# Three-round score visits, table-based roots on ScalarE, and a new recorded order in a two-layer attention and feed-forward kernel

## The chip, the cores and the metric

The kernel runs on one core of a Trainium2 chip. The metric is the time of one execution on the device in microseconds (us). A profile of one execution gives, beside that time, a span: from the first to the last instruction that the profiler recorded. The five engines are named as in the profile: PE (TensorE; its weight loads are listed apart as PEld), DVE (VectorE), ACT (ScalarE), POOL (GpSimd) and SP (SyncE, which here only issues transfers).

## What is computed

Two layers, each of them an attention block and a feed-forward block on 2048 rows of 512 numbers, and both layers with the same weights:

```python
x = x + _A_ref(_layernorm(x), wq, wk, wv, wo, beta)      # attention
x = x + _B_ref(_layernorm(x), w_gate, w_up, w_down)      # gelu(x@w_gate) * (x@w_up) @ w_down
x = x + _A_ref(_layernorm(x), wq, wk, wv, wo, beta)
x = x + _B_ref(_layernorm(x), w_gate, w_up, w_down)
```

The attention has 32 heads of 16 numbers and goes through the rows in four segments of 512. Inside a segment it is causal softmax attention: logits are q times k over 4, those above the diagonal are masked, the softmax is applied to v. Beside it stands a memory: `phi(q) @ M / phi(q) @ z`, where `phi(t)` is `t + 1` for positive t and `exp(t)` else, and M and z gather `phi(k)` and v of the earlier segments. A gate `sigmoid(beta)` for each head mixes the two. The layer norm has no weights: `(x - mean) / sqrt(var + 1e-5)`.

## The kernel before

**Tiling.** A unit of work is one segment of one layer, k = 0 to 7 (k = 0 to 3 are the first layer's segments). Each k has an attention part (class `Att`) and a feed-forward part (class `Ffn`). Everything is kept in SBUF; weights are loaded once. Rows lie 128 to a partition tile, so a segment has four row tiles. A product of 128 x 512 x 512 is four matmuls of 128 columns of weights by 512 columns that gather in one of eight PSUM banks; the down product of the feed-forward part takes 14.

**Two ways to run a product.** `product` (L547 to L559) issues a matmul whole (L559), or as four matmuls of 32 output columns each that run side by side in four quarters of the PE array (L554). The second way, "columns", is taken while the array is already divided like that. Scores need a third way: four heads lie in four groups of 32 rows of the array, and four matmuls of 16 or 32 rows run side by side (L1086), "rows". Each time that the PE goes from one of the three ways to another there is a small gap, and the planner calls that a change of tiling.

**Scores in visits of two rounds.** Each k has 36 rounds of scores. A round is 256 columns in each of four banks, one bank to each of the four row groups. `score` takes two rounds together, a visit: round 0 goes to the first half and round 1 to the second half of four banks. Two exps follow on ACT (L1589), each over two whole banks (128 x 1024). They write probabilities to `pt`, a ring of ten places of one round each. POOL sets the masked probabilities to zero (L1538, L1543), or DVE does by a multiplication (L1548). A flush (L1115) multiplies probabilities by v in columns, and then the places come free. There are 8 x 36 / 2 = 144 visits and 288 exps.

**The layer norm.** In most norms DVE takes mean and variance by two instructions (`bn_stats`, L620, and `bn_aggr`, L623), POOL adds epsilon (L651) and takes the root by a power of -0.5 (L657), DVE writes the normed rows `xn` (L670), and a transposing transfer that SP issues (L520) turns them into `xnT`. For the keys in `BY_PE` (the feed-forward norms of k = 0, 1 and 7) the PE turns them instead (L712, four 128 x 128 transposes for a row tile), and DVE or ACT copies the result out of PSUM. For the three row tiles in `QUICK` (feed-forward norm of k = 1) the sum is taken in the addition itself (`added`, L633), and ACT takes the variance by a Square with a running sum (L640).

**The order.** Nothing is scheduled at run time. While the program is built, `order` runs a planner: it keeps a clock for each engine (class `Clocks` and class `Engine`), with a written duration for each step, and at each point gives the next instruction to the engine whose clock is lowest. Work waits in `items` (PE's products, by due time) and in the engines' `jobs` (by readiness and a slack). A table `POLICY` of some 60 numbers sets due times and slacks, and `STAGES` changes them in stretches of planned time. Each engine then carries out its own instructions in exactly the recorded order and waits at semaphores for the others. Where the planner finds nothing for PE to do but a bank is free, it issues a filler: a 128-column matmul on a tile named `warm` that nobody reads. Twelve of 512 columns also stand at the start, ahead of the first rows.

**The head.** The code before the planner's loop is written by hand: four transfers of x on two queues, statistics of row tiles 0 to 2 on DVE and of row tile 3 on ACT, roots on POOL (L1378), `xn` on DVE, transposes on PE (L722), the first half products of q and k, and the first scores.

## Time and profile before

| what | value |
|---|---|
| median of 3 runs | 537.1 us (536.97 to 538.29) |
| the profiled execution | 536.73 us, span 534.8 us |
| PE busy | 526.8 us of the span |
| DVE, ACT, POOL busy | 432.7, 433.8, 280.2 us |
| granted TensorE clock | 1.00 |

A matmul's duration in the profile holds its way through the array: 512 columns are listed with 380 ns, but in a stream they start some 215 ns apart. So an engine that is listed as busy all the time may still have small gaps in its stream, and a gap of the array is longer than the idle time listed for it. Durations on the other engines also overlap a little from one instruction to the next.

### The profile page before, as it was taken

The page shows a single profiled execution, that of the slowest core. Times are in us where ns is not written, and L with a number is a line of the kernel's source. Part 1 is how long each engine was busy: PE and PEld are TensorE (multiplying, and loading weights), DVE is VectorE, ACT ScalarE, POOL GpSimd, SP SyncE. Part 2 cuts the span into 40 slices and gives each one's busy share as a digit, 9 for nine tenths or more (in the row PEclk, how much of TensorE's full clock was granted, in tenths as well). Part 3 has the DMA queues.
Part 4 walks back from the last instruction along what each step waited for, and adds up shares of the span by engine and source line. Part 5 has one row for each costly group of instructions (what it writes and reads, how often), then busy time and mean ns, then how long its engine had stood idle before and what let it go on. Part 6 is the DMA issues. An engine that isn't in the chain of part 4 may idle for free.

```text
span 534.8 us, 22313 instructions
## 1 busy us (share of the span) xinstructions
PE 526.8 (99%) x9803; PEld 270.1 (51%) x9803; DVE 432.7 (81%) x814; ACT 433.8 (81%) x544; POOL 280.2 (52%) x344
## 2 busy tenths in 40 slices
PE   8999999999999999999999999999999999999997
PEld 4544454555545455545444554545555456545444
DVE  7898899899999998688897889888786797786342
ACT  5999999997998799998999899998879977820320
POOL 4876767385836587337671697816465254100000
PEclk9999999999999999999999999999999999999999
DMA  8345910640122143210130130220231003100001
GB/s 271 67 116 113 242 33 2 171 76 18 34 49 44 24 52 61 43 32 4 43 80 1 26 82 4 42 52 12 63 63 23 1 12 92 24 4 31 11 0 39
DMA packets 72403, 28.83 MB, mean 54 GB/s; under 512 B 56690, under 2 KB 72306, under 8 KB 72306
## 3 DMA queue, kind: packets, MB, share of 16 engines
q1 hardware_dynamic: 72016, 27.15, 23.5%
q8 instruction: 76, 1.25, 1.0%
q10 hardware_dynamic: 290, 0.26, 0.1%
q14 instruction: 21, 0.17, 0.1%
HBM read 9.70 MB, written 2.10 MB: 22 GB/s over the span
## 4 chain that ended last, share of the span: by engine, by line
PE 89%; DVE 5%; ACT 4%; issue 1%; POOL 1%; ACTq 0%; DVEq 0%; POOLq 0%
PE ps L559 43%; PE ps L554 30%; PE ps L1086 8%; PE ps L1115 6%; ACT pt L1589 2%; DVE st L620 1%; DVE gel_sb L1277 0%; ACT wd_sb L545 0%; PE ps L1015 0%; DVE x_sb L1206 0%; DVE byq L1134 0%; DVE e L894 0%; DVE st L1368 0%; DVE xn L670 0%; PE ps L712 0%
## 5 line engine op out<-in xcount | busy, mean ns | idle before, releaser
L1589 ACT ACTIVATE pt<-ps 128x1024 bf16<-128x1024 f32 x288 | 280.3, 1032 | 35.6 <-PE ps L1086 27.2
L1538 POOL TENSOR_SCALAR_AFFINE_SELECT pt<-pt 128x256 bf16<-128x256 bf16 (+1 forms) x192 | 113.9, 606 | 126.5 <-ACT pt L1589 123.1
L1277 DVE TENSOR_TENSOR gel_sb<-gel_sb,ps 128x512 bf16<-128x512 bf16 x112 | 75.6, 683 | 35.6 <-PE ps L559 25.3
L559 PE MATMUL ps<-xnT,wg_sb 128*128 128x512 bf16 x279 | 65.5, 380 | 0.0
L559 PE MATMUL ps<-xnT,wu_sb 128*128 128x512 bf16 x269 | 62.0, 379 | 0.0
L913 POOL TENSOR_SCALAR e<-e 128x512 bf16<-128x512 bf16 x37 | 58.0, 1569 | 2.6 <-ACT e L890 2.0
L1134 DVE STREAM_TRANSPOSE byq<-ps 128x512 f32<-128x512 f32 x64 | 45.3, 707 | 15.5 <-PE ps L1115 14.3
L559 PE MATMUL ps<-wd_sb,gel_sb 128*128 128x512 bf16 (+1 forms) x289 | 56.8, 347 | 0.0
L1206 DVE TENSOR_TENSOR x_sb<-x_sb,ps 128x512 bf16<-128x512 bf16 (+1 forms) x65 | 41.1, 641 | 19.1 <-PE ps L559 15.0
L554 PE MATMUL ps<-wd_sb,gel_sb 128*32 128x512 bf16 (+1 forms) x860 | 49.9, 368 | 0.2 <-issue 0.2
L1543 POOL TENSOR_SCALAR_AFFINE_SELECT pt<-pt 64x1024 bf16<-64x1024 bf16 x28 | 33.4, 1195 | 16.8 <-ACT pt L1589 15.8
L554 PE MATMUL ps<-xnT,wg_sb 128*32 128x512 bf16 x676 | 41.5, 380 | 0.2 <-ACT xnT L545 0.2
L554 PE MATMUL ps<-xnT,wu_sb 128*32 128x512 bf16 x716 | 41.1, 379 | 0.1
L559 PEld LDWEIGHTS <-wg_sb 128*128 128x128 bf16 x279 | 25.7, 98 | 29.7 <-issue 0.9
L559 PEld LDWEIGHTS <-wu_sb 128*128 128x128 bf16 x269 | 25.2, 98 | 29.8 <-issue 0.7
L620 DVE BATCH_NORM_STATS2 st<-x_sb 128x6 f32<-128x512 bf16 x57 | 38.4, 673 | 0.3
L559 PEld LDWEIGHTS <-gel_sb 128*128 128x128 bf16 x289 | 26.8, 98 | 23.2 <-issue 0.9
L1115 PE MATMUL ps<-pt,vaug 128*32 128x256 bf16 (+2 forms) x1344 | 34.8, 238 | 0.0
L544 DVE CAST gel_sb<-ps 128x512 bf16<-128x512 f32 x42 | 28.4, 681 | 6.7 <-PE ps L559 4.0
L1115 PEld LDWEIGHTS <-vaug 128*32 128x32 bf16 x1344 | 27.8, 97 | 10.5 <-issue 1.6
L1336 ACT ACTIVATE gel_sb<-gel_sb 128x2048 bf16<-128x2048 bf16 (+3 forms) x22 | 32.3, 1540 | 0.0
L1086 PEld LDWEIGHTS <-kx 32*128 32x128 bf16 x1120 | 16.6, 92 | 29.0 <-issue 28.4
(152 smaller groups left out, 871.6 us busy)
## 6 DMA issues: line engine op xcount, KB each, us to landing
vz<-vaug SPq DMA_DIRECT2D x14, 136.0 KB, 2.6
wg_sb<-in_B_w_gate_dram SPq DMA_DIRECT2D x8, 224.0 KB, 4.1
wu_sb<-in_B_w_up_dram SPq DMA_DIRECT2D x8, 224.0 KB, 6.4
wd_sb<-in_B_w_down_dram SPq DMA_DIRECT2D x7, 256.0 KB, 4.6
x_sb<-in_A_x_dram SPq DMA_DIRECT2D x3, 512.0 KB, 6.8
out_dram<-x_sb SPq DMA_DIRECT2D x12, 128.0 KB, 1.8
xnT<-xn SPq DMA_TRANSPOSE x48, 2.6
kx<-kf SPq DMA_DIRECT2D x12, 64.0 KB, 2.6
```

The lines of the kernel that those rows point to most:

```text
L554: nc.tensor.matmul(out[r], lhsT=lhsT[:, r], rhs=rhs, start=start, stop=stop, tile_position=(0, 32 * c))
L559: nc.tensor.matmul(out, lhsT=lhsT, rhs=rhs, start=start, stop=stop)
L620: nc.vector.bn_stats(out=self.st6[:, 0, :], in_=x_sb[:, self.tt0 + j, :])
L913: lambda eng: eng.tensor_scalar(out=e[0][:], in0=e[0][:], scalar1=1.0, scalar2=None, op0=ALU.min), summed)
L1086: nc.tensor.matmul(ps_all[:, bank, o + c0:o + c0 + n], lhsT=lhsT, rhs=self.q[rows, b, q0:q0 + n], start=True, stop=True, tile_position=(32 ...
L1115: nc.tensor.matmul(ps()[32 * j:32 * j + 32, q0:q0 + nq], lhsT=va[:, ki * VW + g:ki * VW + g + 32], rhs=pt_all[:, places[t], j, o:o + nq], ...
L1134: nc.vector.transpose(out=(self.byq[:, pars[0], :, :].rearrange("p a c -> p (a c)") if h is None else self.byq[:].rearrange("p u a c -> p ...
L1206: ck.dve.post(ck.made(), slack, (0.15 + 0.00104 * (c1 - c0), lambda: nc.vector.tensor_tensor(out=xt, in0=xt, in1=ps()[:, 0:c1 - c0], op=AL ...
L1277: ck.dve.post(ck.made(), NORMAL, (0.683, lambda: nc.vector.tensor_tensor(out=g, in0=g, in1=ps()[:], op=ALU.mult), lambda t: (ps.read(t), e ...
L1538: nc.gpsimd.affine_select(out=view, in_=view, pattern=[[0, 4], [0, n], [1, C]], compare_op=ALU.is_ge, fill=0.0, base=C, channel_multiplier=-1)
L1543: nc.gpsimd.affine_select(out=view, in_=view, pattern=[[0, 4 * TPS], [1, C]], compare_op=ALU.is_ge, fill=0.0, base=0, channel_multiplier=-1)
L1589: nc.scalar.activation(out=pt_all[:, s0:s0 + 2, 2 * p:2 * p + 2, :].rearrange("p r h c -> p h r c"), in_=ps_all[:, pair[0]:pair[1] + 1, :] ...
```

## The change

**Visits of three rounds.** With the policy number `triple` on, `score` takes three rounds together. They use six banks (three pairs) and three exps of the same size as before. Of the four row groups, two use banks 4, 2, 2 and 5, 3, 3 of the visit's six, and the other two 0, 0, 4 and 1, 1, 5 (`OWN`; `HIGH` tells which half). Two banks are thus written by two different row groups, one half each, and ahead of the first matmul that goes to such a second half PE waits until its earlier matmul to that bank has ended (`clobber_nop`). `triple` is on in three stretches; the built program has 12 visits of three rounds and 126 of two. `pt` has twelve places in place of ten.

**Roots.** `scales` posts the root to both POOL (as before) and ACT, and the engine that comes to it first in the plan takes it. On ACT it is a Ln with epsilon as bias and an Exp with a scale of -0.5, both of 128 x 2 here. A set of function tables that holds both Ln and Exp is loaded where ACT comes back from gelu.

**Norms.** `QUICK` and `BY_PE` are gone. A policy number (`quick`) says for each feed-forward norm how many row tiles take the sum in the addition and the Square on ACT; all feed-forward norms are rooted in pairs of row tiles; numbers `turn_pe` and `turn_last` say which are turned by PE.

**Head.** ACT takes row tile 0's statistics and DVE those of 1 to 3; the roots are Ln and Exp on ACT for three tiles and then one. The four transposes go to four banks, and ACT and DVE copy them out in turn, with a 256-column `warm` matmul after each. Half products of k and q come after all of them.

**Buffers.** `buf` has five places in place of six, `ab`, `mblk` and `zcols` one in place of two, the reciprocal of the softmax sums is written in place, `bd` is bf16, `warm` shares a place. A flush's first part therefore waits for the unit before it to be turned, not the one before that.

**Loads.** The transfers of wo, w_gate and w_up are planned from 18.04 us on (32.0 before), those of w_down from 59.6 (94.0).

**Planner.** ACT's overlap from one instruction to the next is 0.118 us (0.09 before), DVE's 0.075 (0.07). A new counter, `issue`, counts PE's instructions, and lets the PE clock wait if 256 of them were issued faster than 3.7 us after they were asked for. `POLICY` has new numbers in every place, and `STAGES` thirteen stretches in place of four. Fillers multiply `ident` by itself.

In instructions: PE has 9880 matmuls (9803 before). Transposes of `xn` on PE are 112 (64 before), transposing transfers of `xn` 36 (48 before). Fillers are 22 matmuls, 6 whole and 16 as columns (75 before, 15 whole and 60 as columns). Changes of tiling, counted along PE's order, are 300 (299 before). ACT has 24 Squares (3), 32 small root instructions (none), 16 table loads (14), and 10 fewer evictions of 512 columns. DVE has 39 `bn_stats` (60), 24 additions with a sum (3), and 21 more casts out of PSUM. POOL has 16 roots beside the head's as before, now all of 128 x 2 (14 of the 16 were 128 x 4), the head's two are gone, and there are 4 fewer `min` steps.

The head on ACT, ahead of the first exp, before:

```order
L1383 ACT_TABLE_LOAD
L1383 ACTIVATE pt,shift<-x_sb 128x512
L1384 ACTIVATE pt,mv<-x_sb,shift 128x512
L725 ACTIVATE xnT<-ps 128x4x128 x2
L1409 ACTIVATE macc<-ps 128x32
L1410 ACTIVATE tmp_e_134<-ps 128x32
```

and now (`logs` and `rs` are the two steps of the root):

```order
L1519 ACT_TABLE_LOAD
L1520 ACTIVATE pt,shift<-x_sb 128x512
L1521 ACTIVATE pt,mv<-x_sb,shift 128x512
L1513 ACTIVATE logs<-mv,eps 128x3
L1514 ACTIVATE rs<-logs 128x3
L1513 ACTIVATE logs<-mv,eps 128x1
L1514 ACTIVATE rs<-logs 128x1
L859 ACTIVATE xnT<-ps 128x4x128 x2
L1547 ACTIVATE wd_sb<-ps 128x256
```

The statistics moved from row tile 3 to row tile 0, and four root instructions stand ahead of the copies out of PSUM.

ACT where the first feed-forward norm (k = 0) is turned, before (`e` is a step of phi, `xnT` the copy of the turned rows):

```order
L890 ACTIVATE e<-q 128x512
L1589 ACTIVATE pt<-ps 128x2x2x256 x2
L545 ACTIVATE xnT<-ps 128x4x128 x2
L890 ACTIVATE e<-q 128x512
L1589 ACTIVATE pt<-ps 128x2x2x256 x2
```

and now (`junk` is the Square with the running sum, `ve` and `rs` the root):

```order
L1732 ACTIVATE pt<-ps 128x2x2x256
L760 ACTIVATE junk,mv<-x_sb,mv 128x512
L1732 ACTIVATE pt<-ps 128x2x2x256
L760 ACTIVATE junk,mv<-x_sb,mv 128x512
L780 ACTIVATE ve<-mv,eps 128x2
L786 ACTIVATE rs<-ve 128x2
L1732 ACTIVATE pt<-ps 128x2x2x256
L780 ACTIVATE ve<-mv,eps 128x2
L786 ACTIVATE rs<-ve 128x2
L1732 ACTIVATE pt<-ps 128x2x2x256
```

Squares and roots of the norm stand between single exps on ACT's queue, where before there were exps, a step of phi and the copies alone.

PE in the first segment before, between the 10th and the 12th round of scores (v's product between two whole fillers):

```order
L559 LDWEIGHTS warm
L559 MATMUL ps<-warm 128x128
L559 LDWEIGHTS xnT
L559 MATMUL ps<-wv_sb,xnT 128x512
L559 LDWEIGHTS xnT
L559 MATMUL ps<-wv_sb,xnT 128x512
L559 LDWEIGHTS xnT
L559 MATMUL ps<-wv_sb,xnT 128x512
L559 LDWEIGHTS xnT
L559 MATMUL ps<-wv_sb,xnT 128x512
L559 LDWEIGHTS warm
L559 MATMUL ps<-warm 128x128
```

and now the first fillers of the program, which stand after the 34th round:

```order
L428 LDWEIGHTS wd_sb
L428 MATMUL ps<-wd_sb 128x192
L428 LDWEIGHTS ident
L428 MATMUL ps<-ident 128x128
L428 LDWEIGHTS ident
L428 MATMUL ps<-ident 128x128
L428 LDWEIGHTS xnT
L428 MATMUL ps<-wv_sb,xnT 128x512
```

Before, 42 of the 75 filler matmuls stand ahead of the 13th round; now the 22 that are left stand after the 34th, the 44th and the 57th.

The diff, cut to its core:

```diff
-BY_PE = {("xnTf", 0), ("xnTf", 1), ("xnTf", NK - 1)}
-QUICK = {("xnTf", 1): (0, 1, 2)}
-PT_SLOTS = 10
+VISIT = 3
+PARTS = ((1, 4, 2), (2, 5, 2), (0, 6, 5))
+OWN = ((4, 2, 2), (5, 3, 3), (0, 0, 4), (1, 1, 5))
+HIGH = ((0, 0, 1), (0, 0, 1), (0, 1, 1), (0, 1, 1))
+PT_SLOTS = 12
-BUFS = 6
+BUFS = 5
...
-    flush_wait=4.959, piece_slack=35.752, kb_slack=40.713, mem_slack=-52.285, margin=2.0, qk_due=1.503, e_q=-1.996,
+    rs_pool=-16.958, f_urge=-58.138, quick=4, paired=8, turn_pe=8, turn_last=7, w_at=18.04, w_gap=2.197,
...
-        self.act, self.dve, self.pool, self.sp = Engine(0.09), Engine(0.07), Engine(), Engine()
+        self.act, self.dve, self.pool, self.sp = Engine(0.118), Engine(0.075), Engine(), Engine()
...
+    def issue(self, n=2):
+        for _ in range(n):
+            self.issued += 1
+            at = self.issued % CHUNK
+            if at == CHUNK_ASKED:
+                self.fetching = self.pe + FETCH
+            elif at == CHUNK_END:
+                late = max(0.0, self.fetched - self.pe)
...
+                self.pe += late
+                self.fetched = self.fetching
...
         def scales(self, ready, j0, n):
...
+            def moved(on_pool):
...
+                    nc.scalar.activation(out=self.ve[:], in_=var_in, func=ACT.Ln, bias=eps[:])
...
+            def power():
+                nc.scalar.activation(out=rs(), in_=self.ve[:], func=ACT.Exp, scale=-0.5)
...
+            ck.pool.post(ready, slack + pol.rs_pool, (0.25, lambda: moved(True), None), (1.05, second, told), taken=taken)
+            ck.act.post(ready, slack, (0.29, lambda: moved(False), None), (0.29, power, told), table="exp", taken=taken)
...
         def by_pe(self):
-            return self.key in BY_PE or self.key[0] == "xnTa" and self.key[1] <= pol.pe_turns
+            return (pol.turn_last if self.key[1] == NK - 1 else pol.turn_pe) if self.wide else self.key[1] <= pol.pe_turns
...
+                    if crossed and m == 0 and j == 2:
+                        ck.issue(1)
+                        nc.tensor.clobber_nop([nc.tensor.lower_ap(ps_all[:, i, UNIT:L]) for i in crossed])
...
-                              and (n > 0 or unit < 2 or ("turned", unit - 2) in ev),
+                              and (n > 0 or unit < 1 or ("turned", unit - 1) in ev),
...
-                    if j in self.norm.quick:
+                    if j < pol.quick:
                         self.norm.added(j, ps, self.norm.urge(j))
...
-    first_stats(0)
+    nc.scalar.preload_act_table_set("natural_log_exp_and_others")
+    nc.scalar.activation(out=spare[:, 0, :], in_=x_sb[:, 0, :], func=ACT.Copy, scale=-root / D, accum_out=shift[:])
+    nc.scalar.activation(out=spare[:, 1, :], in_=x_sb[:, 0, :], func=ACT.Square, scale=root, bias=shift[:],
+                         accum_out=n0.mv[:, 0, 1:2])
     first_stats(1)
...
+    first_scale(0, 3)
+    first_scale(3, 4)
...
+            places = [(chosen[j], UNIT * r) if n < VISIT else (chosen[OWN[j][r]], UNIT * HIGH[j][r]) for j in range(4)]
+            a.score_round(t, places, chosen[4:] if r == VISIT - 1 else None)
```

381 lines of the change are left out of this document (243 added, 138 removed).

## The prediction

> **What bounds the kernel now.** I read the page's totals first, then the busy times by stage, then PE's timeline at the places where it has idle time, and last the groups. The totals and the chain that ended last:
>
> ```profile
> PE 526.8 (99%) x9803; PEld 270.1 (51%) x9803; DVE 432.7 (81%) x814; ACT 433.8 (81%) x544; POOL 280.2 (52%) x344
> PE 89%; DVE 5%; ACT 4%; issue 1%; POOL 1%; ACTq 0%; DVEq 0%; POOLq 0%
> ```
>
> PE is listed as busy in all but 8.0 of 534.8 us and carries 89% of the chain. So only two things change the time: work that PE gets or loses, and waits of PE. Where the waits lie is seen by stage (busy us of PE, PEld, DVE, ACT, POOL; the cuts are the first scores, the last exp of the second segment and the last exp of all):
>
> ```profile
> 0.00:11.00 11.00, 9.23 (x59) 4.55 (x60) 8.12 (x28) 5.42 (x13) 3.89 (x16) 1.00 0.84 260
> 11.00:113.40 102.40, 100.02 (x1976) 50.86 (x1974) 91.82 (x181) 98.91 (x127) 72.31 (x85) 1.00 0.48 108
> 113.40:461.70 348.30, 347.30 (x7010) 178.61 (x7010) 295.09 (x545) 311.38 (x382) 202.03 (x241) 1.00 0.20 39
> 461.70:534.80 73.10, 70.28 (x772) 36.12 (x760) 37.64 (x65) 18.06 (x26) 1.94 (x3) 1.00 0.07 17
> ```
>
> PE idles 1.77 us in the head, 2.38 in the first two segments, 1.00 in the other six, and 2.82 at the end, where the last rows are added and sent. ACT is busy 97% of the second stage (98.91 of 102.40) and 89% of the third. So in the first two segments ACT is as full as PE, and later it has room. The waits themselves:
>
> ```profile
> 20.68 0.40 PE L554 MATMUL ps<-warm 128*32 128x128 bf16 x16
> 21.82 0.30 PE L554 MATMUL ps<-warm 128*32 128x128 bf16 x8 [0.19 <-ACT wd_sb L545]
> 24.15 0.22 PE L559 MATMUL ps<-warm 128*128 128x128 bf16 x1 [0.16 <-ACT pt L1589]
> 25.07 0.22 PE L559 MATMUL ps<-warm 128*128 128x128 bf16 x1
> 25.57 0.41 PE L1086 MATMUL ps<-wd_sb 16*128 16x64 bf16 x24 [0.28 <-ACT pt L1589]
> 28.54 1.02 PE L559 MATMUL ps<-xnT,wq_sb 128*128 128x512 bf16 x4 [0.68 <-DVE byq L1134]
> ...
> 74.91 0.66 PE L1015 MATMUL ps<-gel_sb,phik 128*32 128x32 bf16 x64 [0.57 <-ACT pt L1589]
> 76.81 1.48 PE L554 MATMUL ps<-xnT,wg_sb 128*32 128x512 bf16 x24 [0.16 <-ACT xnT L545]
> ```
>
> They stand beside fillers, and ACT releases most. A wait is longer than listed: the filler of 25.07 streams for 0.05 us, and the scores behind it start at 25.57, so the array stood for 0.45 us where 0.28 is listed. The rest, 0.17, is the filler's way through the array. Between 11 and 461.7 us I count 14 starts of PE that come over 0.12 us late beside a plain change of tiling, the first at 21.82 and the last at 454.6 (the eight rows above have six of them). So the array loses 3.4 listed (2.38 + 1.00) + 14 x 0.16 = 5.6 us in waits, and what is not in the head or the end cannot give more than that and the fillers.
>
> **The change, part by part.** The sum is made on the profiled execution, 536.73 us (span 534.8 and 1.9 around it), which lies 0.4 under the median of 537.1.
>
> ```profile
> 61.73 0.59 PE L559 MATMUL ps<-wo_sb,aT 128*128 128x512 bf16 x2
> 62.26 0.40 PE L1086 MATMUL ps<-q,kx 32*128 32x64 bf16 x20
> 62.59 2.33 PE L559 MATMUL ps<-wo_sb,aT 128*128 128x512 bf16 x10
> 73.33 1.01 PE L712 MATMUL ps<-ident,xn 128*128 128x128 bf16 x15
> L712 PE MATMUL ps<-ident,xn 128*128 128x128 bf16 x48 | 3.9, 220 | 0.0
> L559 PE MATMUL ps<-warm 128*128 128x128 bf16 x15 | 2.3, 219 | 0.3 <-ACT pt L1589 0.2
> L554 PE MATMUL ps<-warm 128*32 128x128 bf16 x60 | 2.1, 222 | 0.3 <-ACT wd_sb L545 0.2
> L1086 PE MATMUL ps<-q,kf 16*128 16x256 bf16 x224 | 15.9, 273 | 0.0
> L1086 PEld LDWEIGHTS <-kx 32*128 32x128 bf16 x1120 | 16.6, 92 | 29.0 <-issue 28.4
> ```
>
> *Transposes.* 48 more on PE. Fifteen in a row take 1.01 us, the last alone 0.22, so they start (1.01 - 0.22) / 14 = 0.056 apart: 48 x 0.056 = +2.7 us. Their cover is nil, since PE is the bound. The 12 transposing transfers that go free SP's queue, which the stages show waiting for nothing that PE waits for: 0. The copies out of PSUM go to DVE and ACT and are counted there.
>
> *Fillers.* 15 whole ones and 15 sets of four become 6 and 4, 20 fewer at the 0.056 of a 128-column stream: -1.1. Four `warm` matmuls of 256 columns in the head lie in the head's waits: 0.
>
> *Visits of three.* Two products of 0.216 from 61.73 end at 62.16, and the scores start at 62.26; two rounds are 512 columns, 0.21, and end at 62.47 where the next product starts at 62.59. So a visit pays 0.10 + 0.12 = 0.22 us to come and go. 138 visits in place of 144 would save 6 x 0.22 = 1.3, but the order has 300 changes of tiling against 299, since more products lie between columns and whole; I take +0.1. Twelve times PE waits for a matmul that it issued two rounds earlier. A 256-column one takes 0.273, two rounds some 0.21, so 0.06 of it is left, and the next weights (0.092) are then loaded in the open, partly beside the rest. I take 0.1 each: +1.2. The bounds are 0 (all of it over) and 0.22 (as much as leaving the tiling and coming back), 0 to 2.6.
>
> [...]
>
> *Head.* The rows before, from the first statistics to the first scores:
>
> ```profile
> 4.23 0.63 ACT L1383 ACTIVATE pt<-x_sb 128x512 bf16<-128x512 bf16 x1 [0.67 <-DMA x_sb<-in_A_x_dram]
> 3.63 1.22 DVE L1368 BATCH_NORM_STATS2 st<-x_sb 128x6 f32<-128x512 bf16 x2
> 6.44 0.79 POOL L1378 TENSOR_TENSOR rs<-mv,mhalf 128x2 f32<-128x2 f32 x1 [0.31 <-DVE mv L1374]
> 7.27 0.73 DVE L670 TENSOR_SCALAR xn<-x_sb,mv,rs 128x512 bf16<-128x512 bf16 x2 [0.21 <-POOL rs L1378]
> 10.38 0.40 PE L1086 MATMUL ps<-wd_sb 16*128 16x256 bf16 x12 [0.17 <-DVE tmp_e L464]
> L1409 ACT ACTIVATE macc<-ps 128x32 f32<-128x32 f32 x1 | 0.2, 206 | 0.0
> ```
>
> Before, the last `xn` ends at 8.00, held by POOL's second root (0.79). Now DVE's three statistics and their aggregates end near 6.2 as before, two roots of 0.21 on ACT take POOL's place, and DVE writes four `xn` in a row from 6.2: the fourth ends near 7.6. That is 0.4 earlier. The copies are shared evenly by ACT and DVE, and one product of 0.216 is done ahead of the first scores. But the first half products now stand behind all four transposes. I take -0.5, with 0 (the products' new place takes it all) and -1.0 (both gains whole) as bounds.
>
> *ACT.* What it gets and loses, by these rows:
>
> ```profile
> L640 ACT ACTIVATE junk<-x_sb,mv 128x512 bf16<-128x512 bf16 x3 | 2.2, 723 | 1.4 <-DVE mv L637 1.4
> L640 ACT ACTIVATION_READ_ACCUMULATOR junk<-x_sb,mv 128x1 f32 x3 | 0.6, 187 | 0.0
> L545 ACT ACTIVATE gel_sb<-ps 128x512 bf16<-128x512 f32 x30 | 18.1, 616 | 3.4 <-PE ps L554 2.8 <-PE ps L559 0.3
> L1253 ACT ACTIVATE gel_sb<-ps 128x512 bf16<-128x512 f32 x30 | 15.8, 604 | 0.1
> L1589 ACT ACT_TABLE_LOAD x6 | 7.7, 1283 | 0.1
> 10.82 3.77 ACT L1589 ACTIVATE pt<-ps 128x1024 bf16<-128x1024 f32 x4 [0.18 <-PE ps L1086]
> L1589 ACT ACTIVATE pt<-ps 128x1024 bf16<-128x1024 f32 x288 | 280.3, 1032 | 35.6 <-PE ps L1086 27.2 <-POOL pt L1538 4.7 <-POOL pt L1543 1.2
> ```
>
> 21 Squares x 0.91 = 19.1; 32 root steps x 0.21 = 6.7; 2 table loads = 2.6; 10 evictions fewer, -6.2; 5 gelus out of PSUM fewer, -3.0, but 2.1 more in the wide gelus. That is 21.3 us in 40 more instructions, and four exps in 3.77 us start (3.77 - 1.03) / 3 = 0.91 apart, so each hides 0.12 of itself: 21.3 - 4.7 = 16.6 us. Up to the 72nd exp, the end of the second stage, the new order has 2 Squares, 10 root steps, 2 evictions, a masked copy and half a gelu tile more, 6.1 - 1.8 = +4.3. There ACT idled 3.49, and PE's own work to that point grows by some 3 us (ten down products of 0.216 stand earlier, 32 transposes more, 15 fillers fewer). 3.5 + 3 - 4.3 leaves 2.2 us of room in 105: just enough, and I cost it at 0. In the six later segments the other 12.3 go into 36.9 us of idle time: 0. If that cover is gone, PE waits for the exps, and behind them for PSUM banks.
>
> *DVE, POOL, SP.* An addition with a sum replaces an addition and a statistic; 21 more casts come; in all DVE stays under 83% and POOL under 53%. One `ab` in place of two lets a flush wait for the unit before it: transpose 0.71 twice, reciprocal 0.35, scale 0.72 and second transpose 0.70 make some 3.2 us, and a unit comes every 14 us. 0 each.
>
> *Waits.* Fillers mark the places where the planner had nothing to give. 22 of 75 are left, so I let 71% of the 5.6 us go: -4.0. At nothing given, 0; at all, -5.6.
>
> The sum: +2.7 - 1.1 + 0.1 + 1.2 - 0.5 - 4.0 = -1.6, that is 536.73 - 1.6 = 535.1 us, 0.3% under the own time and 0.4% under the median.
>
> **The rivals.** *ACT takes over as the bound (slower).* Place: the first two segments above all. ACT must run there at (98.91 + 4.3) / (102.4 + 3) = 98%; before it ran at 97% with PE waiting 2.4 us listed. If it keeps its 3.5 us of idle time in the second stage, the 72nd exp comes 4.3 later while PE has only 3 more to do, 1.3 of new wait, and if each of the other six segments loses 0.5 in the same way, 3.0. With none of the old waits given back: 536.73 + 2.4 (the sum without waits) + 4.3 = 543.4; with half of them, 540.6. It decides from 2.4 us of new waits on beside the old ones half kept. For it: ACT's 97% and the 0.57 and 0.28 us that PE waited for exps. Against: ACT has 36.9 us free later.
>
> *The waits come back elsewhere (no change).* Fillers go but PE waits at other semaphores for as long: -4.0 shrinks to -2.5, and 536.6 follows. For it: seven of the 14 waits have no filler beside them.
>
> *All of it goes (faster still).* -5.6 in waits, -1.0 in the head, crossings at 0.05: 536.73 + 2.7 - 1.1 + 0.1 + 0.6 - 1.0 - 5.6 = 532.4. Against: the order is fixed ahead, and 14 late starts came under the old plan too.
>
> *Transposes that do not stream.* If each of the 48 took its whole 0.220 (the L712 group), they would cost 10.6 in place of 2.7, and 543.0 would follow. The start distance of 0.056 and the clock of 1.00 in all four stages speak against it. [...]
>
> **How the numbers follow.** Chances: the forecast 0.49, faster still 0.12, waits elsewhere 0.17, ACT as the bound 0.19, transposes 0.03. A difference under 0.3% (1.6 us) cannot be told from none. The forecast lies just beyond that under the median, and its own range is 532.9 to 536.3: -5.6 and 0.6 for the crossings at the low end, half the waits kept at the high end. Of its 0.49 I give 0.41 to faster and 0.08 to the same; with the 0.12 that makes 0.53. Same: 0.08 and 0.14 of the waits elsewhere, 0.22. Slower: 0.22 for ACT and the transposes and 0.03 from the waits, 0.25. The range goes from 531.8, under the 532.4, to 540.6, ACT as the bound with half the waits; above it and below it some 0.2 are left out.
>
> **What would show it.** Right: PE's idle time by stage under 1.2 us up to the 72nd exp and under 0.6 in the next six segments; transposes still 0.056 apart; the first scores near 9.9 us; at twelve places a start some 0.1 us late inside a visit. Wrong: exps back to back with PE waiting for `pt` or the banks in the first two segments (ACT as the bound); waits of PE for DVE in `byq` (one `ab`); late landings of `kx` and `vz`, since the loads of the weights are planned 14 us earlier, in a stage where the transfers are already 0.48 busy.

## The result, and the profile after

The changed kernel takes 542.98 us (median of 4 runs, 542.05 to 544.6) against 537.45 for the kernel before in the same session: ratio 1.0104, 95% interval 1.0076 to 1.0132. It is slower by 1.0%, 5.6 us, where 1.6 us less was forecast. The profiled execution took 542.96 us with a span of 541.2. From its page, the totals and the chain that ended last:

```profile
PE 524.8 (97%) x9816; PEld 274.6 (51%) x9880; DVE 438.2 (81%) x840; ACT 451.9 (83%) x605; POOL 273.5 (51%) x341
PE 79%; ACT 11%; DVE 3%; DMA 3%; issue 3%; POOL 0%; ACTq 0%; DVEq 0%
```

PE carried 89% of the chain before and ACT 4%; now it is 79% and 11%, with 3% for transfers. ACT's busy time is 451.9, near what the working had (433.8 + 16.6 = 450.4). The trace lacks 64 of the 9880 matmuls (x9816 against x9880 weight loads), which makes PE look less busy than it is. The same four stages as before (cut at the first scores, the last exp of the second segment, the last exp of all):

```profile
0.00:10.40 10.40, 8.41 (x61) 4.71 (x62) 7.45 (x25) 6.31 (x16) 2.15 (x14) 1.00 0.83 253
10.40:116.10 105.70, 103.00 (x2111) 53.90 (x2116) 95.72 (x193) 103.21 (x141) 68.97 (x85) 1.00 0.43 100
116.10:466.40 350.30, 341.92 (x6959) 179.38 (x7004) 299.20 (x560) 317.66 (x412) 201.23 (x241) 1.00 0.21 37
466.40:541.20 74.80, 71.42 (x707) 36.66 (x704) 35.85 (x66) 24.69 (x38) 1.09 (x2) 1.00 0.05 15
```

The head is 0.6 shorter, the second stage 3.3 longer (105.70 against 102.40), the third 2.0 longer (350.30 against 348.30), the end 1.7 longer (74.80 against 73.10). These lengths mislead, because the stages no longer hold the same work. I count PE's stream in the trace of e2, a kernel below with the same PE stream and no record missing. The second stage holds 91.6 us of it against 88.6 before, so it got the 3 us more that the ACT step assumed; the third holds 308.8 against 311.7, the end 70.1 against 68.8. What is left beside the stream and 0.125 us for each change of tiling (explained below) is 4.7 us in the second stage before and in e2 alike, but 9.1 before and 14.1 in e2 in the third. So the loss lies in the six later segments, and not in the first two.

PE idles 2.70 us in the second stage, where under 1.2 was to be seen, but holes of the missing records are in that: in e2 it is 1.26, and 2.82 in the third stage, where under 0.6 was to be seen. PE's waits in the changed kernel, by what ended them (us in all, times, longest):

```profile
PE ps L428 <- issue: 5.3, 32, 0.4
PE ps L428 <- DMA phik<-e: 2.0, 2, 1.7
PE ps L428 <- ACT pt L1732: 0.4, 2, 0.3
```

Most of the 5.3 for "issue" are holes left by the missing records; e2 lists 1.0. New is the 2.0 for `phik`, the transposed `phi(k)` that updates the memory. Its place, in PE's timeline and in the chain:

```profile
115.87 0.24 PE L428 MATMUL ps<-vaug,phik 128*32 128x32 bf16 x12
117.81 0.56 PE L428 MATMUL ps<-vaug,phik 128*32 128x32 bf16 x52 [1.70 <-DMA phik<-e]
```

```profile
112.85 4.91 DMA phik<-e
```

PE needs `phik` 3 us after SP asked for it, and it comes after 4.91.

**PE's time split.** I add up PE's stream and compare with the starts. Matmuls of 512 columns start 0.216 us apart in the median of both traces; this count takes 1.4% less for them, so some 6 us of each kernel's stream stand among its gaps, and what it shows is the difference between kernels. The last matmul starts at 531.7 before and at 537.8 now, 6.1 later. The stream grew from 475.1 to 477.0, by 1.9. The other 4.2 are gaps. From each score visit to the next I take the time, less the stream, less 0.125 for each change of tiling (about the median of both traces). What is left is 13.6 us before and 18.4 now. Some 2.0 of the 18.4 are the crossings, seen inside visits. In the mean a visit of two runs 0.034 over its stream and a visit of three 0.255, which would be 0.22 for a crossing, but two of the twelve (at 429.7 and 458.8 us) have other waits in them, which stay in e1. In the median it is 0.026 and 0.198, so 12 x 0.17. The rest, 16.4, are waits as before (and those 6 us of stream), 2.8 more than the 13.6. The forecast had 4.0 fewer.

The waits beside the fillers (21 to 28 us, and 73 to 77) are indeed mostly gone: by the same measure they were 3.4 us and are 0.8. Others stand elsewhere: 2.17 at 113.4 (the `phik` above), 0.71 at 80.1, 0.87 at 85.5, 0.72 at 280.8, 0.65 at 354.4.

On ACT the group of exps shows the other side; before it read 280.3 busy and 35.6 idle ahead of exps:

```profile
L1732 ACT ACTIVATE pt<-ps 128x1024 bf16<-128x1024 f32 x288 | 276.3, 1053 | 21.6 <-PE ps L428 18.6 <-POOL pt L1672 0.8 <-issue 0.7
```

ACT now stands idle ahead of its exps for 21.6 us only. An exp with no idle time ahead of it starts when ACT comes to it, and not when its scores are there; there are more of these now (243 of 288, before 206).

### The profile page after: what moved, and what is told of

It is laid out like the page before. It is cut to its first block, busy times and chain, and to the rows that moved or that the text cites. A ratio compares the mean times of both kernels' runs of the same rounds, so it can differ in the third digit from the quotient of the medians.

```text
span 541.2 us, 22448 instructions
## 1 busy us (share of the span) xinstructions
PE 524.8 (97%) x9816; PEld 274.6 (51%) x9880; DVE 438.2 (81%) x840; ACT 451.9 (83%) x605; POOL 273.5 (51%) x341
## 3 DMA queue, kind: packets, MB, share of 16 engines
q8 instruction: 77, 1.26, 1.0%
## 4 chain that ended last, share of the span: by engine, by line
PE 79%; ACT 11%; DVE 3%; DMA 3%; issue 3%; POOL 0%; ACTq 0%; DVEq 0%
PE ps L428 78%; ACT pt L1732 8%; DMA phik<-e 2%; ACT gel_sb L1474 1%; PE ps L432 1%; DMA amT<-am 1%; DVE byq L1273 1%; DMA x_sb<-in_A_x_dram 1%; DVE ab L1288 0%; ACT L470 0%; ACT gel_sb L1391 0%; DVE st L1507 0%; ACT e L1025 0%; DVE gel_sb L662 0%; DVE aT L1295 0%
## 5 line engine op out<-in xcount | busy, mean ns | idle before, releaser
L1732 ACT ACTIVATE pt<-ps 128x1024 bf16<-128x1024 f32 x288 | 276.3, 1053 | 21.6 <-PE ps L428 18.6
L1672 POOL TENSOR_SCALAR_AFFINE_SELECT pt<-pt 128x256 bf16<-128x256 bf16 (+1 forms) x192 | 113.4, 604 | 125.6 <-ACT pt L1732 119.4
L428 PE MATMUL ps<-wd_sb,gel_sb 128*32 128x512 bf16 (+3 forms) x1138 | 104.2, 359 | 2.1 <-issue 1.4
L428 PE MATMUL ps<-xnT,wg_sb 128*32 128x512 bf16 (+1 forms) x924 | 103.8, 379 | 2.4 <-issue 1.4
L428 PE MATMUL ps<-xnT,wu_sb 128*32 128x512 bf16 (+1 forms) x1007 | 101.2, 379 | 1.6 <-issue 1.6
L428 PEld LDWEIGHTS <-gel_sb 128*32 128x32 bf16 (+1 forms) x1344 | 51.9, 97 | 41.1 <-issue 2.7
L428 PEld LDWEIGHTS <-wu_sb 128*32 128x32 bf16 (+1 forms) x1018 | 44.3, 97 | 46.6 <-issue 1.1
L428 PEld LDWEIGHTS <-wg_sb 128*32 128x32 bf16 (+1 forms) x943 | 42.3, 97 | 45.0 <-issue 2.7
L428 PE MATMUL ps<-xnT,wq_sb 128*32 128x512 bf16 (+2 forms) x254 | 33.2, 377 | 0.9 <-ACT pt L1732 0.3
L428 PE MATMUL ps<-xnT,wk_sb 128*32 128x512 bf16 (+2 forms) x257 | 33.4, 376 | 0.3 <-ACT kf L663 0.2
L428 PE MATMUL ps<-q,kx 32*128 32x64 bf16 (+2 forms) x1120 | 32.1, 217 | 0.6 <-issue 0.4
L428 PE MATMUL ps<-wv_sb,xnT 128*32 128x512 bf16 (+1 forms) x257 | 31.1, 380 | 0.7 <-issue 0.3
```

The source lines that it names most:

```text
L428: return self.nc.tensor.matmul(*args, **kw)
L1672: nc.gpsimd.affine_select(out=view, in_=view, pattern=[[0, 4], [0, n], [1, C]], compare_op=ALU.is_ge, fill=0.0, base=C, channel_multiplier=-1)
L1732: nc.scalar.activation(out=probs.rearrange("p r h c -> p h r c"), in_=ps_all[:, pair[0]:pair[1] + 1, :].rearrange("p h (r c) -> p h r c", ...
```

## The experiments

All were timed in five rounds beside the kernel before. Since its median moved by 0.7 us between sessions, I compare ratios; a difference of 0.001 is 0.54 us, and the intervals are about 0.0014 to each side. Unless it is said otherwise an edit keeps the recorded order word for word, so only the named instructions change. Two theories stood at the start: the time went into work and waits of PE that can be priced one by one (crossings, transposes, the late `phik`), or ACT had become the bound.

### One thing taken away at a time

No crossings (e1), and kx transfers of a quarter (e2):

```diff
-                        nc.tensor.clobber_nop([nc.tensor.lower_ap(ps_all[:, i, UNIT:L]) for i in crossed])
...
             places = [(chosen[j], UNIT * r) if n < VISIT else (chosen[OWN[j][r]], UNIT * HIGH[j][r]) for j in range(4)]
+            if n == VISIT and r == VISIT - 1:
+                places[2:] = [(chosen[0], UNIT), (chosen[1], UNIT)]
...
-                        out=kx[r:r + 16, :, C:3 * C], in_=kf[r:r + 16, :, :]), told))
+                        out=kx[r:r + 16, 0:4, C:3 * C], in_=kf[r:r + 16, 0:4, :]), told))
```

> The changed kernel with its order kept, but in the twelve visits of three the third round of row groups 2 and 3 is written to these groups' own banks (over their second round) and not to the banks of groups 0 and 1, and the wait ahead of it is gone. The third-round scores of these two groups are thus left out. PE has as many matmuls as before. If a crossing costs what the trace of the changed kernel shows inside its visits (0.255 us over the stream, against 0.034 in a visit of two, so 0.22 each), the time falls by 12 x 0.22 = 2.6 us against the changed kernel's 543.0, to 540.4. If a crossing costs the 0.1 of the prediction: by 1.2, to 541.8. If ACT is the bound (PE only waits later for exps): by under 0.5.

> The changed kernel with its order kept, but each of the twelve transfers that send the odd heads' keys into kx copies four of its sixteen tiles (16 KB in place of 64), so three quarters of these keys are left out of the scores. Theory: PE's wait of 1.7 us for phik at 115.9 comes from phik's transposing transfers being queued with the four kx transfers that were issued just ahead of them; then phik lands some 2 us earlier, the wait goes, and the time falls by 1.5 to 2.2 us, to 541. Rival (the transposes are late of themselves, or issued late): phik still lands 4 to 5 us after its issue, and the time changes by under 0.5. Rival (ACT as the bound in the first two segments, where it is 97.6% busy): phik lands early, the wait is gone from PE's list, but the time falls by under 0.5.

e1: 542.49 us, ratio 1.0097 (1.0082 to 1.0113). The visits did get shorter, as one visit of three shows, in the changed kernel and in e1:

```profile
435.01 0.68 PE L428 MATMUL ps<-q,kx 32*128 32x64 bf16 x20
```

```profile
434.91 0.51 PE L428 MATMUL ps<-q,kx 32*128 32x64 bf16 x20
```

0.17 us less for each, 2.0 for twelve. But the end moved by 0.4, less than the intervals can tell from nothing. At another visit the time saved turned into a wait behind it:

```profile
447.12 0.40 PE L428 MATMUL ps<-q,kx 32*128 32x64 bf16 x20
447.83 0.63 PE L428 MATMUL ps<-pt,vaug 128*32 128x256 bf16 x24 [0.31 <-DVE x_sb L1343]
```

In the changed kernel the same flush starts at 447.78, behind a longer visit and without a wait:

```profile
447.30 0.56 PE L428 MATMUL ps<-q,kx 32*128 32x64 bf16 x20
447.78 0.63 PE L428 MATMUL ps<-pt,vaug 128*32 128x256 bf16 x24
```

e2: 542.84 us, 1.0112 (1.0099 to 1.0126). PE's wait for `phik` is listed with less than the 2.0 us of the changed kernel, and the time is the same:

```profile
PE ps L428 <- DMA phik<-e: 0.7, 1, 0.7
```

The trace of e7 (below), with whole kx transfers, has the same line. The landing itself says little about its cause: `phik` lands after 3.3 us in the median in the changed kernel, 2.6 in e2, but also 3.3 in e1 and 2.5 in e3, whose kx transfers are whole. That the kx transfers hold it up is not shown. In the kernel before the landing takes 2.4 in the median and 5.7 at most, and PE waits for none: the last of these transfers in the second stage is asked for at 105.71 us there, and the product that reads it starts at 118.09. So the new order also leaves a landing less time, 3 us in place of 12.

48 transposes fewer (e3), and all three edits (e4):

```diff
             ops += [(Clocks.MM[128], whole(lambda kt=kt: te.transpose(
-                turned()[:, kt, :], xn()[:, kt * P:(kt + 1) * P], ident[:]))) for kt in range(KT)]
+                turned()[:, kt, :], xn()[:, kt * P:(kt + 1) * P], ident[:]) if kt < 2 else ck.issue())) for kt in range(KT)]
```

> The changed kernel with its order kept, but of the four PE transposes of each of 24 row tiles only two are issued, and the copy out of PSUM writes these two twice. So 48 transposes are gone (half of the normed rows are wrong in these tiles), and all else stays. If transposes stream 0.056 us apart: 48 x 0.056 = 2.7 us less, 540.3. If each takes its whole 0.22: 10.6 less, 532.4. If ACT is the bound: under 0.5 less.

> The three edits above in one kernel (no crossings, short kx transfers, 48 transposes fewer), order kept. If PE is the bound and the three are independent: 2.6 + 2 + 2.7 = 7.3 us less than the changed kernel, 535.7, which is under the kernel before (537.4). If ACT is the bound in the first two segments, or behind PE everywhere: no more than the largest single one of the three and 540 or more.

e3: 541.94 us, 1.0101 (1.0082 to 1.0121). e4: 541.72, 1.0095 (1.0081 to 1.0109). Work and waits of PE that were expected to be worth 7.3 us were taken out, and 0.5 came back, which the intervals don't tell from nothing. The trace of e4 shows where it went: PE's stream is 2.6 us shorter than in e2 and the crossings are gone, but what is left beside stream and changes of tiling is 20.0 us against 18.9 in e2. So PE's stream alone does not set the time. Next, ACT: exps of 768 elements in place of 1024, in the changed kernel (e5) and in the one before (e6), and small Squares (e7).

```diff
+        few = UNIT if rounds[0][0] == 0 and rounds[0][1] < PT_SLOTS else UNIT * 3 // 4
...
-                    out=probs.rearrange("p r h c -> p h r c"),
-                    in_=ps_all[:, pair[0]:pair[1] + 1, :].rearrange("p h (r c) -> p h r c", r=2), func=ACT.Exp, scale=SCALE)
+                    out=probs.rearrange("p r h c -> p h r c")[:, :, :, 0:few],
+                    in_=ps_all[:, pair[0]:pair[1] + 1, :].rearrange("p h (r c) -> p h r c", r=2)[:, :, :, 0:few], func=ACT.Exp, scale=SCALE)
...
-                nc.scalar.activation(out=junk[:], in_=xt, func=ACT.Square, scale=float(D) ** -0.5, bias=self.mv[:, j, 0:1],
+                nc.scalar.activation(out=junk[:, 0:32], in_=xt[:, 0:32], func=ACT.Square, scale=32.0 ** -0.5, bias=self.mv[:, j, 0:1],
```

> The changed kernel with its order kept, but each exp of scores after the first twelve rounds handles 192 of the 256 columns of a round (768 elements for each partition in place of 1024), so a quarter of the probabilities are old ones. An exp takes 1.03 us, a 512-column one 0.61, so this one takes about 0.82, and ACT has some 270 x 0.21 = 57 us less to do. Theory (ACT's stream, not PE's work, sets the pace through most of the changed kernel, and what PE is spared comes back as waits for exps): the time falls by at least 5 us, to 538 or less, and the waits of PE over a plain change of tiling (18.4 us in the changed kernel) fall to under 12. Rival (the waits come from elsewhere: DMA, PSUM banks in the order, DVE): the time falls by under 1.5.

> The kernel before with the same cut of its exps (after the first ten rounds). Theory (ACT paces the changed kernel, PE the one before): it falls by less than the changed kernel does, by 1 to 3 us of its 537.0. If ACT paces both alike: it falls by as much as the changed kernel. If neither: by under 1.

> The changed kernel with its order kept, but the 24 Squares with running sum on ACT read 32 of 512 columns, so the variances are those of 32 columns. A Square falls from 0.72 to some 0.25 us, 24 x 0.47 = 11 us less on ACT, all of it at places that the change brought. Theory (ACT's stream sets the pace, and the Squares that the change puts between the exps are what lengthens it): 2 to 8 us less than the changed kernel's 543.0, since two thirds of the Squares lie in segments where ACT is over 95% busy. If ACT has room: under 1 less.

e5: 541.51 us, 1.0091 (1.0077 to 1.0104). e6: 536.43, 0.9992 (0.9983 to 1.0001). e7: 542.88, 1.0116 (1.0102 to 1.0130). In e5 the exps and the chain read:

```profile
L1733 ACT ACTIVATE pt<-ps 128x768 bf16<-128x768 f32 (+1 forms) x288 | 219.8, 818 | 56.2 <-PE ps L428 50.9 <-issue 1.6 <-POOL pt L1672 1.4
```

```profile
PE 89%; DVE 7%; DMA 2%; issue 1%; POOL 1%; ACT 0%; DVEq 0%; POOLq 0%; ACTq 0%
```

56 us less in the exps (50 less of ACT's busy time, 402.1) took ACT out of the chain altogether (0%), and the time fell by 0.7 by the ratios. So ACT alone does not set it either. Both simple theories fell: neither engine is the bound by itself.

### Both together

Short exps, and on top of them no crossings (e19), half the transposes (e20), or all three edits of PE (e10):

> The changed kernel with the short exps (192 of 256 columns) and the three earlier edits of PE's stream and waits together: no crossings, kx transfers of a quarter, 48 transposes fewer. Theory of two streams (PE and ACT are both near full, so that easing the one shows the other; each alone gave 0.1 to 1.5 us): eased together they give what each was expected to give alone, 541.5 - 12 x 0.17 - 2.7 = 536.8 or less, no longer slower than before. Rival (a third thing bounds both: DVE, the transposing transfers, or PE's supply of instructions): 539.5 or more.

> The changed kernel with short exps (541.5) and no crossings, its transposes and kx transfers as they are. If PE is the bound then, and a crossing costs the 0.17 us by which the visits of three got shorter without it (0.52 to 0.35): 12 x 0.17 = 2.0 less, 539.5. By the prediction's 0.1: 1.2 less, 540.3. If other waits close up behind the crossings: under 0.7 less.

> The changed kernel with short exps (541.5) and 48 transposes fewer, its crossings and kx transfers as they are. If PE is the bound then: 48 x 0.056 = 2.7 less, 538.8. If half of them stand beside waits, as the doubled transposes in the kernel before (1.4 for 48): 1.4 less, 540.1. If other waits close up behind them: under 0.7 less.

e10: 538.31 us, 1.0027 (1.0017 to 1.0037). e19: 540.21, 1.0063 (1.0050 to 1.0076). e20: 541.89, 1.0093 (1.0077 to 1.0109). The same three edits that gave 0.5 with full exps (e4) give 3.4 with short ones (1.0091 to 1.0027), between the two values expected for e10. All of it together gives 4.1, where the edits of PE alone gave 0.5 and the short exps alone 0.7. The crossings, worth nothing measurable before, are now worth 1.5 (1.0091 to 1.0063). This fits two streams that are both nearly full: what is eased on one waits for the other. The transposes by themselves still gave nothing. The trace of e20 has one stall of 1.1 us that no semaphore explains (last section), but e5 has 1.8 us of such stalls in all; it also lists 0.9 us of PE's waits for exps, where e5 lists none of 0.15 us or more. Why they gave nothing stays open.

What is left over the kernel before in e10 was tried on two suspects: DVE (e15), and the late `phik`, by letting the update read another tile (e16).

```diff
-                        out=g, in0=g, in1=ps()[:], op=ALU.mult),
+                        out=g[:, 0:384], in0=g[:, 0:384], in1=ps()[:, 0:384], op=ALU.mult),
...
-                    te.matmul(pairs()[32 * c:32 * c + 32, b, :], lhsT=self.phik[:, j, b * P + 32 * c:b * P + 32 * c + 32],
+                    te.matmul(pairs()[32 * c:32 * c + 32, b, :], lhsT=self.kf[:, j, b * P + 32 * c:b * P + 32 * c + 32],
```

> The changed kernel with short exps and PE's three edits (538.3), and also the 112 multiplications of gelu by up on DVE done for 384 of 512 columns (the other columns keep the gelu alone), some 112 x 0.14 = 15 us less on DVE. If DVE (81% busy, 88 to 92% in six of eight segments) is the third bound: 1.5 us less or more, 536.8. If not: under 0.5 less.

> The changed kernel with short exps and PE's three edits (538.3), and the update of the memory multiplies k itself (kf) in place of phi(k), so PE no longer waits for the transposing transfers that bring phik; these are still made. The memory is thus wrong. In the profile of the 538.3 kernel PE stands 2.1 us at 110.9 and 1.0 us at 164.8 at these products, over a plain change of tiling. If these waits are then on the path: 2 to 3 us less, 535.3 to 536.3. If something else holds PE right behind: under 1 less.

e15: 537.83 us, 1.0017 (1.0009 to 1.0026), 0.5 less than e10, which the intervals don't separate. e16: 537.30, 1.0006 (0.9995 to 1.0017), 1.1 less, under half of what PE stood there in e10's trace.

So there is a ladder from the changed kernel down to the one before. Each line has the edits of the line above and one more:

```
changed kernel                               1.0104
  exps of 768 in place of 1024 (e5)          1.0091   -0.7 us
  no crossings (e19)                         1.0063   -1.5
  48 transposes fewer, kx a quarter (e10)    1.0027   -1.9
  no wait for phik (e16)                     1.0006   -1.1
kernel before, exps of 768 (e6)              0.9992
```

The last two lines still differ, and e16 has 0.6 us less of PE's stream than e6 (473.7 and 474.4). Its waits, by the measure of 13.6 and 18.4 above, are 15.5 us, and 13.7 in e6. So some 1.4 us (0.8 of time and 0.6 of stream; an estimate, for the intervals do not separate the two times) lie in waits of the new order that none of these edits takes away.

Last, the Squares in place of the exps as the relief of ACT (e14, to be held against e4 without it and e10):

> The changed kernel with full exps, but the 24 Squares read 32 of 512 columns (11 us less on ACT) and PE's three edits are made (no crossings, kx transfers of a quarter, 48 transposes fewer). With the Squares at full width the three edits gave 541.7. If the Squares and small roots that the change puts on ACT are what holds PE's savings back: 538 to 539.5, near the 538.3 with short exps. If ACT's load is spread over all exps and the Squares lie in its idle time: 541 to 542.

e14: 541.98 us, 1.0093 (1.0077 to 1.0108), the same as e4. In the new order, cutting the Squares frees nothing, even with PE eased. A likely reading is that they stand where the plan had kept room for them; no run shows it.

### The parts added to the kernel before

21 Squares that nobody reads (e8), every planned transpose issued twice (e12), both (e13), the Squares with short exps (e18), and the fillers left out (e9):

```diff
                 nc.vector.bn_stats(out=self.st6[:, 0, :], in_=x_sb[:, self.tt0 + j, :])
+                if self.key[0] == "xnTf" and self.key[1] != 1 and j < 3:
+                    nc.scalar.activation(out=junk[:].rearrange("p (a c) -> p a c", c=P), in_=wide, func=ACT.Square, accum_out=more[:])
...
+            def both(kt):
+                for _ in range(2):
+                    nc.tensor.transpose(turned()[:, kt, :], xn()[:, kt * P:(kt + 1) * P], ident[:])
...
-                product(ps()[:, 0:P], warm[:], wide[:, 0, :])
```

> The kernel before with its order kept and 21 Squares with running sum of 512 columns added on ACT, each where DVE begins the statistics of a row tile of a feed-forward norm (row tiles 0 to 2 of every such norm but that of k = 1). They read a constant tile and nothing reads them, so they cost ACT's time alone, 21 x 0.79 = 16.6 us. Theory (ACT has too little room for the change's additions): 3 to 10 us more than before's 537.0, so that this part alone would do as much as the whole change (+5.6). If ACT's idle time takes them in, as the prediction had it: under 1 more.

> The kernel before with its order kept, but each of the 48 transposes of normed rows on PE that its planner placed is issued twice, the second writing the same values: 48 more on PE, as many as the change adds, and no other work. If PE is the bound of the kernel before and transposes stream: 48 x 0.056 = 2.7 us more, 539.5. If their cover is waits behind other engines: under 1 more. If they take 0.22 each: 10.6 more.

> The kernel before with its order kept and both additions: the 48 doubled transposes on PE and the 21 added Squares on ACT (which alone gave +3.5). If the two loads add up: 3.5 plus what the doubled transposes give alone, up to 6.2, so 540.3 to 543, about the whole loss of the change (+5.6). If they hide each other: no more than 3.5 more, 540.3.

> The kernel before with its order kept, the 21 Squares added on ACT, and the short exps (which alone gave 536.4 against 536.8). If the added Squares cost 3.5 us through ACT's time: with 57 us less of exps they cost under 0.7, so 536.4 to 537.1. If they cost through the places where they stand (each delays the exp behind it by 0.8 us, however much room ACT has): 538.5 to 540.

e8: 540.32 us, 1.0069 (1.0056 to 1.0081), +3.7. e12: 538.12, 1.0033 (1.0021 to 1.0046), +1.8. e13: 541.50, 1.0086 (1.0073 to 1.0099), +4.6. e18: 536.06, 0.9980 (0.9972 to 0.9989); it is not slower than e6. In e8, the added Squares, the exps, and PE's wait for exps at the scores (L1089; the row of L1086 is the kernel before's):

```profile
L623 ACT ACTIVATE junk<-warm x21: 621/629/663, 66.5 to 476.8; 128x512 bf16<-128x512 bf16 x21
L623 ACT ACTIVATION_READ_ACCUMULATOR junk<-warm x21: 186/200/235, 67.0 to 477.4; 128x1 f32 x21
```

```profile
L1592 ACT ACTIVATE pt<-ps 128x1024 bf16<-128x1024 f32 x288 | 281.1, 1032 | 29.0 <-PE ps L1089 23.2 <-POOL pt L1541 2.8 <-POOL pt L1546 1.2
```

```profile
PE ps L1086 <- ACT pt L1589: 0.7, 2, 0.4
PE ps L1089 <- ACT pt L1592: 2.4, 6, 0.6
```

21 x (0.63 + 0.20) = 17 us of listed instructions, 12 us of ACT's busy time because they overlap (445.6 against 433.8), took 6.6 us of the idle time ahead of the exps (35.6 to 29.0) and lengthened the kernel by 3.7. With short exps (e18) the same Squares cost nothing, so it was ACT's time and not the places where they stand. The kernel before had no spare ACT time where it was needed, though its page shows ACT busy for 81% of the span. The transposes cost two thirds of their stream of 2.7.

> The kernel before with its order kept, but without the 75 filler matmuls (15 whole, 15 sets of four) that the planner placed; no result depends on them. The prediction's step: these stand where the planner had nothing else, and with them go their own 30 x 0.056 = 1.7 us and some of the waits. If fillers lengthen PE's stream: 1.7 us less than before's 536.8, 535.1. If they only lie in time in which PE would wait for ACT, DVE or a bank anyway: under 0.5 less, and the waits beyond a plain change of tiling (13.6 us in the kernel before) grow by what the fillers took.

e9: 536.33 us, 0.9992 (0.9983 to 1.0001). 75 matmuls gone, 1.7 us of stream, and 0.4 of time, which the interval does not tell from nothing. The gaps over plain changes of tiling grew from 13.6 to 14.7, and PE's waits for exps went from 0.7 in two places to 1.3 in four:

```profile
PE ps L1086 <- ACT pt L1589: 1.3, 4, 0.6
```

The fillers stood inside waits. Without a filler the wait is still there.

## Why the prediction was wrong

The forecast was 535.1, the time 543.0, above the range that ended at 540.6. PE's stream came out near the forecast (+1.9 against the +1.6 of transposes and fillers); its waits did not. By steps:

- **Waits (-4.0): wrong, and the main failure.** The step took the fillers as the measure of the waits. The changed kernel shows that they are not: its fillers went from 75 to 22, and the waits rose by 2.8 beside the crossings. What was gained where the fillers had stood (2.6) came back twice over elsewhere, most of it in the six later segments. e9 shows from the other side that a filler is not what PE waits for: taking all of them out leaves the waits standing. A filler says that the planner had no work at that place; what PE waits for on the chip is another matter. The sum is off by 6.8 here. The rival "the waits come back elsewhere" named this, but let only 1.5 of the 4.0 come back.
- **ACT (0): wrong.** The working had 2.2 us of room in the first two segments and 36.9 idle later, and let 16.6 more vanish in it. The time idle was not room: 35.6 us of it lay ahead of exps, 27.2 until their scores came, and what is put between exps there delays the next one. The added Squares alone cost +3.7 in the old order (e8), through ACT's time (e18). In the new order the load shows differently: no relief of ACT alone gives more than 0.7 (e5), and none gives anything through the Squares (e7, e14), but with ACT relieved PE's own additions come to light. It also depends on the stage: short exps (e5) take what is left beside stream and changes of tiling from 4.7 to 3.5 us in the second stage, but only from 14.1 to 13.7 in the third, where the loss lies.
- **Transposes (+2.7): rate right, weight less.** Sixteen in a row start (1.07 - 0.22) / 15 = 0.057 apart, so the rival in which they don't stream is out:

```profile
71.98 1.07 PE L432 MATMUL ps<-ident,xn 128*128 128x128 bf16 x16
```

  Of their 2.7, 1.8 reached the end in the old order (e12).
- **Crossings (+1.2): mechanism right, size too small.** 0.17 in the median of the trace and by e1's visits, against the 0.1 that was taken and within the bound of 0.22. In most of the twelve visits the first matmul behind the wait starts 0.10 to 0.13 us after the listed end of the last one of the visit's first round, and its weights (0.092) begin to load only after that end, where the step let them run partly beside the rest. 12 x 0.17 = 2.0 of PE's time, of which 1.5 reach the end once ACT is out of the way (e19).
- **Fillers (-1.1): too large.** All 75 are worth 0.4 (e9), so 20 of the 30 sets nearly nothing.
- **Changes of tiling (+0.1): right**, 299 to 300.
- **Head (-0.5): direction right.** The first scores start at 10.18 against 10.38, where 9.9 was to be seen, with one product more done ahead of them (0.2). In the traces of the changed kernel's variants it is 9.94 to 10.33, in those of the kernel before's 10.39 to 10.49:

```profile
10.18 0.40 PE L428 MATMUL ps<-wd_sb 16*128 16x256 bf16 x12 [0.17 <-DVE cden L580]
```

- **DVE (0): no loss shown** (e15, 0.5 within the intervals). The wait for `phik` was in no step; it costs 1.1 once PE and ACT are eased (e16).

The rival "ACT takes over as the bound" had the sign and the time (540.6 to 543.4), but only half of the mechanism, and most of the loss is not at its place: by itself ACT is worth 0.7 of the 5.6, and the first two segments have in all as much waiting as before (4.7 by the same measure). The kernel before was already held by two engines at once (work added to either lengthens it, e8 and e12; easing either gives 0.4, e6 and e9), and the change put more on both, 18 us on ACT and some 4 on PE (1.9 of stream, 2.0 of crossings). From below, Squares and transposes together make +4.6 of the 5.6 (e13); from above, relieving both streams and the `phik` wait takes 5.3 back (e16), though by cutting ACT's exps by more than the change had added. The new places of all the other instructions, and the smaller buffers, were not tested by themselves. Of the signs named, late landings of `kx` came (4.1 us in the median against 2.6), but PE lists no wait for them, and its waits for `byq` are 0.2 us each.

Open stays what PE waits for in the six later segments. Of the 5.0 us more there (9.1 to 14.1), 1.7 are crossings (ten of the twelve) and some 1.3 the late `phik` (12.3 in e10, 11.0 in e16); short exps return 0.4. Open also is why the cut Squares return nothing in the new order where short exps return 3.4 together with PE's edits; the exps were cut by five times as much (50 us of ACT's busy time against 9). And open is why some landings of `phik` take 5 us. No kernel here beats the one before by more than its measurement can tell, apart from those that leave exps out.

## What to carry to other kernels

Idle time of an engine, summed over a stage, is not room (35.6 us of it lay ahead of the exps here, and 12 us of added work cost 3.7): look at what stands behind it in the queue, and test it by adding useless work there, as e8 does for little. When two engines are nearly full, taking load off one may show nothing (0.5 on PE in e4, 0.7 on ACT in e5, 4.1 on both in e10), and pricing terms one by one (or undoing them one by one) misleads; ease both at once and then put back the parts. Fillers mark where a planner had no work, not where the chip waits (0.4 for all 75 in e9).

## What was unexpected of the hardware

**Stalls of PE at one place in 256 instructions.** PE has stalls that no semaphore explains, and they come at instructions whose number in PE's program (weight loads included) leaves 193 to 196 when divided by 256. In the 19 traces that lack no record, every idle time of PE over 0.15 us that is put down to "issue", the head left out, stands at such a number. In e5, 256 instructions apart (17859 and 18115):

```profile
452.49 0.40 PE L428 MATMUL ps<-q,kf 16*128 16x256 bf16 x12
453.37 0.52 PE L428 MATMUL ps<-q,kf 16*128 16x256 bf16 x4 [0.48 <-issue]
...
457.09 0.19 PE L428 MATMUL ps<-q,kx 32*128 32x64 bf16 x2
457.97 0.21 PE L428 MATMUL ps<-q,kx 32*128 32x64 bf16 x4 [0.69 <-issue]
```

And in e3, in the midst of one product (3010):

```profile
86.42 0.83 PE L428 MATMUL ps<-xnT,wg_sb 128*32 128x512 bf16 x11
88.40 0.83 PE L428 MATMUL ps<-xnT,wg_sb 128*32 128x512 bf16 x12 [1.15 <-issue]
```

I looked at these boundaries in ten of these traces (before, e2, e3, e4, e5, e7, e8, e10, e16, e20), each by the time that PE took for the 256 instructions up to it; a stall is a gap over 0.15 us beyond the usual distance of such matmuls:

```
the 256 instructions took   boundaries   with a stall
under 4 us                  112          18 (0.18 to 1.32 us)
4 to 5 us                   114           2 (0.22, 0.30)
over 5 us                   513           0
```

So in these traces PE stalls only where it gets through 256 instructions in under 5 us, as it does where scores and columns stand close, and there at 20 of 226 boundaries. Per trace it comes to 0.7 us in the kernel before, 1.4 in e2 (the changed kernel's PE stream) and 1.8 in e5. A saving may vanish in this way: at 3010 the 256 instructions took 4.36 us in e2, with a stall of 0.3, and with fewer transposes 3.65 in e3, with one of 1.3 (e20: 3.64 and 1.1). But it is no fixed price: e4 and e10, with the same transposes gone, stall there for 0.4 and 0.2 only. e16, which also has them gone, stalls there for 1.1 us, and for 1.5 in all.

Transfers of instructions come at the same distance. The page of the changed kernel lists

```profile
q8 instruction: 77, 1.26, 1.0%
```

77 transfers of 1.26 MB in all, 16 KB each. PE's program has 19,799 entries, 257 to a transfer. In the trace of the kernel before the 76 transfers of this queue start while PE is at its entries 175 to 19,353, in the mean 256 apart. That a stall is a wait for such a transfer is my reading and not shown: no run here slowed or hastened one, and none is under way in the stall from 174.65 to 174.87 us in the kernel before (the last one ended at 173.49, the next starts at 175.97).

**Two row groups in one PSUM bank.** Handing half of two banks from one row group to another inside a visit, with the wait that stands ahead of it, costs PE 0.17 us each time (0.68 to 0.51 above), more than a change of tiling (0.125 by the count above).
